# Route steps at fixed places of an attention unit: PSUM banks, product order and engine changed together

## The chip, the cores and the metric

One core of a Trainium2 chip runs the whole program. The metric is the device time of one launch in microseconds (us); lower is better. Engines are named as the profile names them: PE (TensorE, products; PEld its weight loads), DVE (VectorE), ACT (ScalarE), POOL (GpSimd), SP (SyncE, which here issues transfers). Each runs its own instructions in program order.

## What is computed

Three blocks follow each other (the reference, cut):

```python
# 1 attention: 2 batches, 8 heads, 768 positions, head size 64
keep = is_global | is_local                    # 8 global keys, 96 local ones
scores = where(keep, scale*q@k.T + bias, -1e9)
a = exp(scores - max); a = a / (sum(a) + 1e-09)
x = a @ v
# 2 a sequential route and one of 8 experts for each token
fresh_e = argmax(logits[b, s])
e = fresh_e if s == 0 or local_gate < 0.5 else prev_e
out[b, s] = softmax(logits)[e] * (relu(x @ w1[e]) @ w2[e])
# 3 real part of a 2-D FFT, norm and a two-layer MLP
```

The expert of a token can be that of the token before it, so the route of a tile of 128 positions needs the last state of the tile before.

## The kernel before

**Units.** Attention runs in `fast_attention` as 24 units, `n` = 0 to 23: six tiles `i` of 128 queries, two batches `b`, two groups `g` of four heads, `n = 4i + 2b + g`. A unit has at most 256 keys. Its work is spread over four rounds of the main loop. Round `n` issues in this order: `out(n-2, 1)` (ACT copies the second half of the turned probabilities, L165), `keep(n-3)` (DVE copies the values' sums from PSUM, L178), `scores(n)` (PE, L132), `rowmin(n)` (DVE, four L141), `upright(n-3)` (PE, L183: two products that turn the sums upright and give the gate logits), `norm(n-3)` (DVE, L195 to L201), `step` (slot 0), `transp(n-1, 0)` (PE, L159), `expo(n)` (ACT, four L150), `out(n-1, 0)`, `step` (slot 1), `transp(n-1, 1)`, `step` (slot 2), `values(n-2)` (PE, L173), `step` (slot 3). Where this text says unit `n`, the stretch from the start of `scores(n)` on PE to that of `scores(n+1)` is meant.

**Route.** After the fourth unit of a tile, `norm` adds the generator `Route.run` to the background. Each `step` advances every background generator to its next `yield`, so the number of `yield`s alone decides in which slot a route step is issued, and it does so for all but the last tile while later units run. The steps are: sum of the logits (`lg`, L465), maximum and index (L490, L493), gate masks `gn` and `gf` (L491, L497), two products that turn them into rows (L501, L502, into `rp`), ACT copy of the rows (L508), exponentials and their sum (L503, L505), a scan along the tokens (`ex`, L512), the one-hot `oh` (L517), a counting scan (`cu`, L521), products for the counts of other tiles (`other`, L531, L532), the rank `rk` (L539), two products for the places (`pp`, L544, L545), their cast (`pos`, L549), a store of the rows to memory on SP (L552) and on POOL two indirect scatters of the token list (L553). Tile 3 goes on: SP reads the first 128 list entries (L564), POOL gathers their rows with an indirect DMA (`x0`, L567).

**PSUM.** `values` writes columns 256 to 511 of the bank `sm` (`turned`); `rp` is in columns 0 to 255 of that bank. `upright` writes columns 0 to 295 of the bank `mi` (`back`); `other` and `pp` are in columns 304 to 310 of `mi`. The recording layer orders accesses of one bank's tile.

**Splits.** Four generators `Ring.take` (table `TAKES`) split expert weights into two parts while units 12 to 24 run: for each 128x512 piece ACT casts it (L991) and POOL subtracts (L993, `eng=lambda: G`). There are 16 pieces.

**Afterwards.** `early` runs an MLP for the 128 gathered tokens on PE (L825, L839 to L855) while the last tile's route ends; then lists are read and the experts start (L1088).

Of the kernel before, what the change touches and what calls it, by code (L numbers as in the profile page):

```python
# [11 lines left out]
F32 = mybir.dt.float32  # L12
# [5 lines left out]
AF = mybir.ActivationFunctionType  # L18
ALU = mybir.AluOpType
# [4 lines left out]
P = 128  # L24
B, H, S, D = 2, 8, 768, 64
E, F = 8, 1024
DM = H * D
NT = S // P
# [12 lines left out]
GATE = -1.5 * 2.0 ** -23  # L41
# [19 lines left out]
def fast_attention(tc, st, io, route):  # L61
    nc = tc.nc
    V, A, G, T = nc.vector, nc.scalar, nc.gpsimd, nc.tensor
    KS = 3
    HP = B * H // 2
    with ExitStack() as ctx:
# [79 lines left out]
        def expo(n):  # L146
            u = live[n]
            u.den = wk.tile([P, 4], F32, name="den", bufs=4)
            for x in range(4):
                A.activation(u.t[:, x, :u.W], u.t[:, x, :u.W], AF.Exp, bias=u.nm[:, x:x + 1], scale=-1.0, accum_out=u.den[:, x:x + 1])  # L150

# [35 lines left out]
        def norm(n):  # L187
# [69 lines left out]
        def step(k):  # L257

            for at, g, lo, hi in TAKES:
                if k == at:  # L260
                    bg.add(st.ring.take("e", g, cols=512, follow=False, part=(lo / 4, hi / 4), eng=lambda: G))
            bg.step()
            for _ in range(AHEAD.get(k, 0)):
                next(ahead, None)

        for n in range(N + 3):
# [35 lines left out]
            if ok(n - 1):  # L302
                transp(n - 1, 1)
            step(k + 2)
            if ok(n - 2):
# [8 lines left out]
        for k in range(4 * 3, max(AHEAD) + 1):  # L314
            step(k)
            if k == LOAD:
                st.ring.load(PIECES)
        bg.drain()
        for _ in ahead:
# [104 lines left out]
class Route:  # L424
    def __init__(self, tc, st, io):
        self.tc, self.st, self.io = tc, st, io

    def pools(self, ctx, turn=True):
# [19 lines left out]
    def run(self, i, xs, parts=None):  # L448
# [10 lines left out]
        rp = sm[:16, :256]  # L459
        pp = mi[:, 304:304 + B]  # L460
        other = mi[:16, 308:309]
        from2, from1 = st.pairs[:16, 0:16], st.pairs[:16, 16:32]
# [3 lines left out]
        else:  # L466
# [8 lines left out]
            A.copy(lg, lp)  # L475
        yield
        l8 = lg[:, :, :E]
# [18 lines left out]
        V.tensor_tensor(pe, l8, m8[:, :, :1].to_broadcast([P, B, E]), op=ALU.subtract)  # L496
# [5 lines left out]
        T.matmul(rp[:, P:2 * P], gf.rearrange("p b e -> p (b e)"), self.identb, start=True, stop=True)  # L502
        A.activation(pe, pe, AF.Exp)  # L503
        yield
        V.tensor_reduce(out=su, in_=pe, op=ALU.add, axis=AX.X)  # L505
        yield
        rows = sb.tile([16, P], F32, name="rows")
        A.copy(rows, rp[:, :P])  # L508
        V.tensor_scalar(su, su, 1e-9, None, op0=ALU.add)
        yield  # L510
        ex = sb.tile([16, P], F32, name="ex")
        V.tensor_tensor_scan(ex, rows, rp[:, P:], 0.0 if i == 0 else st.pe[:, P - 1:],  # L512
                             op0=ALU.mult, op1=ALU.add)
        V.reciprocal(su, su)
        yield
        oh = sb.tile([16, P], F16, name="oh")
        V.tensor_scalar(oh, ex, st.eid, None, op0=ALU.is_equal)  # L517
        yield
        cu = sb.tile([16, P], F32, name="cu")
# [3 lines left out]
        st.pe, st.pc = ex, cu  # L523
        yield
        if i < NT - 1:

            yield
            yield

        if i > 0:  # L530
            T.matmul(other, from2, before[:, P - 1:], start=True, stop=False)  # L531
        T.matmul(other, from1, cu[:, P - 1:], start=i == 0, stop=True)  # L532
        if i == NT - 3:
            less = mi[:1, 310:311]
# [3 lines left out]
        yield  # L538
        V.scalar_tensor_tensor(rk, cu, other, oh, op0=ALU.add, op1=ALU.mult)  # L539
        for b in range(B):  # L540
            V.tensor_scalar(xs[b][:, DM:DM + E], pe[:, b], su[:, b], None, op0=ALU.mult)
        yield
        yield
        T.matmul(pp, rk, st.sel, start=True, stop=False)  # L544
        T.matmul(pp, oh, st.base, start=False, stop=True)  # L545
        yield
        yield
        pos = sb.tile([P, B], I32, name="pos")
# [1260 lines left out]
```

## Time and profile before

| | |
|---|---|
| median of 3 runs | 680.07 us (678.15 to 684.28) |
| the profiled execution: its own time | 676.13 us |
| its span, first to last instruction | 674.2 us |
| PE / DVE / ACT / POOL busy | 627.2 / 400.3 / 279.4 / 88.4 us |
| TensorE clock granted, mean | 0.981 |

A line of the page's groups names source line, engine, operation, output and input, sizes and count, then busy time, mean of one, and the idle time in front with what ended it. A timeline row has the start from the span's beginning, the duration, the engine, line, operation and in brackets the idle time in front of it and its releaser. Instructions of one engine overlap at their ends, so the step from start to start is what one costs.

### The profile page before, as it was taken

How to read it: one execution, taken by the hardware profiler on the slowest of the kernel's cores; microseconds unless marked ns; L12 is line 12 of the kernel's file. 1: busy time of each engine (PE TensorE's matmuls, PEld its weight loads, DVE VectorE, ACT ScalarE, POOL GpSimd, SP SyncE). 2: the span in 40 equal slices, each digit the busy share in tenths (PEclk: the TensorE clock that was granted, in tenths of full speed). 3: DMA queues.
4: the chain of work that ended last, by engine and by line, in shares of the span. 5: the costliest groups of instructions: out<-in, count | busy, mean ns of one | idle time of the engine just before them, and what ended most of it. 6: DMA issues, size and time to landing. Idle time of an engine off the chain costs nothing.

```text
span 674.2 us, 9953 instructions
## 1 busy us (share of the span) xinstructions
PE 627.2 (93%) x3621; PEld 511.7 (76%) x3622; DVE 400.3 (59%) x939; ACT 279.4 (41%) x562; POOL 88.4 (13%) x100
## 2 busy tenths in 40 slices
PE   8987877687999999999999899999999999999997
PEld 3665665457899889888777688777778888888886
DVE  3767777732986598866158986989641141244112
ACT  6766668212655566655343453442211131131110
POOL 0003334423043213231010000000000000000000
PEclk8999999896999999999999999999999999999999
DMA  8332344316888887896144134245010010100001
GB/s 305 130 113 79 129 135 90 113 39 250 290 290 333 321 273 258 339 367 214 64 175 173 35 113 165 92 163 181 1 64 0 1 63 1 63 0 1 0 1 62
DMA packets 25217, 92.47 MB, mean 137 GB/s; under 512 B 7660, under 2 KB 8812, under 8 KB 17216
## 3 DMA queue, kind: packets, MB, share of 16 engines
q1 hardware_dynamic: 19408, 77.44, 33.3%
q0 software_dynamic: 4736, 10.56, 4.2%
q10 hardware_dynamic: 1008, 3.65, 1.5%
q8 instruction: 35, 0.57, 0.4%
q14 instruction: 30, 0.25, 0.1%
HBM read 81.03 MB, written 14.84 MB: 142 GB/s over the span
## 4 chain that ended last, share of the span: by engine, by line
PE 38%; DVE 11%; ACT 2%; issue 1%; DMA 1%; DVEq 0%; ACTq 0%
PE h L1621 16%; PE acc L1637 5%; PE acc L1635 5%; PE acc L1636 5%; DVE dec L1017 1%; DVE dec L1019 1%; PE y L1126 1%; PE more L1176 1%; PE more L1126 1%; PE h L1176 1%; DVE dec L1015 1%; DVE dec L1013 1%; DMA u<-x 1%; PE f L1587 1%; DVE wide L971 1%
## 5 line engine op out<-in xcount | busy, mean ns | idle before, releaser
L1626 DVE SCALAR_TENSOR_TENSOR hl<-h,hh 128x512 fp32r<-128x512 f32 x48 | 33.1, 689 | 118.5 <-ACT hh L1625 118.5
L1625 ACT ACTIVATE hh<-h 128x512 fp32r<-128x512 f32 x48 | 28.7, 597 | 153.8 <-PE h L1621 153.7
L993 DVE TENSOR_TENSOR wide<-raws,wide 128x1024 fp32r<-128x1024 f32 (+1 forms) x38 | 45.0, 1200 | 24.2 <-ACT wide L991 23.9
L150 ACT ACTIVATE t<-t,nm 128x256 f32<-128x256 f32 (+1 forms) x96 | 45.9, 480 | 21.9 <-DVE nm L141 21.8
L991 ACT CAST wide<-raws 128x1024 fp32r<-128x1024 f32 (+2 forms) x46 | 43.3, 957 | 6.1 <-PE acc L1637 3.4
L1621 PE MATMUL h<-un0h,wide 128*128 128x512 f32 (+1 forms) x136 | 42.4, 378 | 0.1
L141 DVE CUSTOM_DVE_ANT_0 t<-sp,bias 128x256 f32<-128x256 f32 (+1 forms) x96 | 32.8, 398 | 9.9 <-PE sp L132 7.9
L1636 PE MATMUL acc<-wide,hh 128*128 128x512 f32 x96 | 37.7, 393 | 0.0
L1635 PE MATMUL acc<-wide,hh 128*128 128x512 f32 x96 | 37.7, 393 | 0.0
L1637 PE MATMUL acc<-wide,hl 128*128 128x512 f32 x96 | 37.5, 391 | 0.0
L173 PE MATMUL sm<-p,vs 128*64 128x128 f32 x352 | 25.7, 288 | 5.3 <-ACT rows L508 5.3
L1149 ACT ACTIVATE hh<-h 128x512 fp32r<-128x512 f32 x28 | 16.7, 597 | 31.1 <-PE h L1146 23.2
L1621 PEld LDWEIGHTS h<-un0h,wide 128*128 128x128 f32 x136 | 25.0, 188 | 5.0 <-ACT un0h L1397 0.3
L1146 PE MATMUL h<-xh,wide 128*128 128x256 f32 x192 | 28.4, 284 | 0.4 <-DVE hl L1150 0.3
L165 ACT COPY p<-tp 128x512 f32<-128x512 f32 (+1 forms) x48 | 24.8, 538 | 8.5 <-PE tp L159 8.5
L1056 POOL DMA_INDIRECT xg<-xs,ent x23 | 25.8, 1120 | 15.9 <-issue 6.1
L173 PEld LDWEIGHTS sm<-p,vs 128*64 128x64 f32 x352 | 19.7, 142 | 9.9 <-ACT rows L508 6.5
L1146 PEld LDWEIGHTS h<-xh,wide 128*128 128x128 f32 x192 | 25.5, 192 | 1.2 <-ACT sl5h L991 0.5
L1150 DVE SCALAR_TENSOR_TENSOR hl<-h,hh 128x512 fp32r<-128x512 f32 x28 | 19.2, 686 | 11.9 <-ACT hh L1149 9.7
L159 PE MATMUL tp<-consts,t 128*128 128x128 f32 x176 | 25.7, 287 | 0.2
L1621 PE MATMUL h<-un0l,wide 128*128 128x512 f32 (+1 forms) x68 | 25.6, 377 | 0.0
L183 PE MATMUL mi<-iw,o 128*128 128x148 f32 x96 | 18.8, 320 | 5.9 <-DVE o L178 5.0
(447 smaller groups left out, 1665.7 us busy)
## 6 DMA issues: line engine op xcount, KB each, us to landing
raws<-we SPq DMA_DIRECT2D x30, 1024.0 KB
raws<-wm SPq DMA_DIRECT2D x17, 1024.0 KB
raws<-wmf SPq DMA_DIRECT2D x7, 1024.0 KB
wmf<-dec POOLq DMA_DIRECT2D x8, 512.0 KB
xs<-xrow SPq DMA_DIRECT2D x12, 260.0 KB
vs<-v SPq DMA_DIRECT2D x6, 512.0 KB
raws<-kq SPq DMA_DIRECT2D x3, 1024.0 KB
u<-x SPq DMA_DIRECT2D x6, 512.0 KB
```

The costliest lines, as they stand in the source:

```text
L141: V.tensor_tensor_reduce(out=u.t[:, x, :u.W], in0=u.sp[:, j, k, :u.W], in1=bias[:, 4 * u.g + x, u.b0:u.b0 + u.W], scale=-0.125, scalar=3.0 ...
L150: A.activation(u.t[:, x, :u.W], u.t[:, x, :u.W], AF.Exp, bias=u.nm[:, x:x + 1], scale=-1.0, accum_out=u.den[:, x:x + 1])
L173: T.matmul(turned[j * D:j * D + D, k], vs[:, ti % KS, u.h + 2 * k + j], u.p[:, 2 * k + j, c], start=c == 0, stop=c == len(tiles) - 1)
L991: (first or nc.scalar.copy)(hi[:, cs], raw[:, cs])
L993: (eng() if callable(eng) else eng or nc.vector).tensor_tensor(lo[:, cs], raw[:, cs], hi[:, cs].bitcast(F32), op=ALU.subtract)
L1146: T.matmul(ps[:, u], w[:, f], x[:, k], start=n == 0, stop=n == 11)
L1621: nc.tensor.matmul(ps[:, c], a[:, k], x[:, k, c], start=n == 0, stop=n == 11)
L1625: nc.scalar.activation(hh, ps, AF.Relu)
L1626: nc.vector.scalar_tensor_tensor(hl, ps, 0.0, hh.bitcast(F32), op0=ALU.max, op1=ALU.subtract)
L1635: T.matmul(acc[c], hh[:, cs], h2, start=first, stop=False)
L1636: T.matmul(acc[c], hh[:, cs], l2, start=False, stop=False)
L1637: T.matmul(acc[c], hl[:, cs], h2, start=False, stop=last)
```

## The change

It does five things. `upright(n-3)` and `norm(n-3)` are issued behind `transp(n-1, 1)` instead of behind `scores(n)` (except in the last two rounds). `pp`, `other` and `less` lie in the bank `sm` (columns 0 to 6) instead of `mi`. Route steps name a slot to be issued in (`at`, `to`), except those of the last tile; both row products' results are copied by one ACT copy right behind the products. Six small steps go from DVE to POOL: the `+ 1e-9` of the attention's denominators (once a unit), and for all tiles but the last `gn`, the subtraction for `pe`, the `+ 1e-9` of `su` and the two scalings of `xs`. The 16 subtractions of the splits go from POOL to DVE.

```diff
         def expo(n):
...
+            G.tensor_scalar(u.den, u.den, 1e-9, None, op0=ALU.add)
...
-            V.tensor_scalar(rs, u.den.unsqueeze(2), 1e-9, None, op0=ALU.add)
-            V.reciprocal(rs, rs)
+            V.reciprocal(rs, u.den)
...
-                    bg.add(st.ring.take("e", g, cols=512, follow=False, part=(lo / 4, hi / 4), eng=lambda: G))
+                    bg.add(st.ring.take("e", g, cols=512, follow=False, part=(lo / 4, hi / 4)))
+            route.slot = k % 4
...
-            if ok(n - 3):
+            if ok(n - 3) and not ok(n - 1):
                 upright(n - 3)
                 norm(n - 3)
...
                 transp(n - 1, 1)
+                if ok(n - 3):
+                    upright(n - 3)
+                    norm(n - 3)
...
+    def at(self, s, n=1):
+
+        for _ in range(1 if s is not None else n):
+            yield
+        while s is not None and self.slot not in (None, s):
+            yield
...
-        pp = mi[:, 304:304 + B]
-        other = mi[:16, 308:309]
+        pp = sm[:, 0:B]
+        other = sm[:16, 4:5]
+        last, soon = i == NT - 1, i in (NT - 3, NT - 2)
+        X = V if last else G
+        to = lambda s, n=1: self.at(None if last else s, n)
...
-        V.tensor_scalar(gn, z.to_broadcast([P, B, E]), GATE, None, op0=ALU.is_ge)
+        X.tensor_scalar(gn, z.to_broadcast([P, B, E]), GATE, None, op0=ALU.is_ge)
...
-        yield
-        yield
+        yield from to(0, 2)
         T.matmul(rp[:, 0:P], gn.rearrange("p b e -> p (b e)"), self.identb, start=True, stop=True)
...
+        if not last:
+            A.copy(rows, rp)
...
+        X.tensor_scalar(su, su, 1e-9, None, op0=ALU.add)
...
-        yield
-        if i < NT - 1:
-
-            yield
-            yield
-
+        yield from to(3)
         if i > 0:
             T.matmul(other, from2, before[:, P - 1:], start=True, stop=False)
...
-        yield
-        yield
+        yield from to(3, 2)
         T.matmul(pp, rk, st.sel, start=True, stop=False)
```

Three places in the program, as the order of instructions has them. First PE in unit 13, before: `scores`, the two `upright` products (L183), the route's `other` (L531, L532), the transposes, the values.

```order
L132 MATMUL sp<-raws 128x256 x4
L183 MATMUL mi<-iw,o 128x148 [waits DVE_49]
L183 MATMUL mi<-iw,o 128x148
L531 MATMUL mi<-cu,consts 16x1 [waits DVE_49]
L532 MATMUL mi<-cu,consts 16x1
L159 MATMUL tp<-consts,t 128x128 [waits Activation_49]
```

The same unit on PE after (L184 is `upright`, L174 the values, L546 and L547 are `other`):

```order
L132 MATMUL sp<-raws 128x256 x4
L160 MATMUL tp<-consts,t 128x128 [waits Activation_49]
L160 MATMUL tp<-consts,t 128x128 x3
L160 MATMUL tp<-consts,t 128x128 [waits Activation_49]
L160 MATMUL tp<-consts,t 128x128 x3
L184 MATMUL mi<-iw,o 128x148 [waits DVE_49]
L184 MATMUL mi<-iw,o 128x148
L174 MATMUL sm<-p,vs 64x128 x8
L546 MATMUL sm<-cu,consts 16x1
L547 MATMUL sm<-cu,consts 16x1 [waits DVE_49]
```

`other` moved from the second place of the unit to its end and out of the bank that `upright` writes; `upright` moved behind the transposes.

Second DVE in unit 13, behind the four L141, before (L539 is `rk`, L541 the scaling of `xs`, L178 the next `keep`):

```order
L195 TENSOR_SCALAR rs<-den 128x4
L196 RECIPROCAL rs<-rs 128x4 [waits DVE_49]
L199 TENSOR_TENSOR lgp<-mi,rs 128x40 [waits DVE_49,PE_49]
L201 TENSOR_TENSOR xrow<-mi,rs 128x256
L539 SCALAR_TENSOR_TENSOR rk<-cu,mi,oh 16x128 [waits PE_49]
L541 TENSOR_SCALAR xrow<-pe,su 128x8 x2
L178 COPY o<-sm 128x256 [waits PE_49]
```

And after (L541 is now `cu`, L1009 a split, L555 `rk`, L179 `keep`):

```order
L541 SCALAR_TENSOR_TENSOR cu<-consts,cu,oh 16x128 [waits DVE_49]
L1009 TENSOR_TENSOR sl0l<-raws,sl0h 128x512 [waits DMAHW6_49,Activation_49]
L196 RECIPROCAL rs<-den 128x4
L199 TENSOR_TENSOR lgp<-mi,rs 128x40 [waits DVE_49,PE_49]
L201 TENSOR_TENSOR xrow<-mi,rs 128x256
L555 SCALAR_TENSOR_TENSOR rk<-cu,sm,oh 16x128 [waits PE_49]
L1009 TENSOR_TENSOR sl0l<-raws,sl0h 128x512 [waits Activation_49]
L179 COPY o<-sm 128x256
```

Two splits and the counting scan joined the unit; the small addition and the two scalings left it.

Third POOL around unit 22, before (L553 are tile 3's scatters, L567 the gather of `x0`, L993 splits, L104 a patch of keys):

```order
L553 DMA list<-dest,pos 12416x2 [waits DVE_49]
L553 DMA list<-dest,pos 12416x2
L993 TENSOR_TENSOR wide<-raws,wide 128x512 [waits Activation_49]
L993 TENSOR_TENSOR wide<-raws,wide 128x512 [waits DMAHW4_49,Activation_49]
L104 COPY kq<-gk 128x4x8 [waits PE_49]
L567 DMA vs<-xs,ent_89 128x520 [waits DMAHW3_49,DMAHW5_49,DMAHW2_49,DMAHW6_49,DMAHW1_49,DMAHW7_49,DMAHW0_49,DMASW0_49]
L993 TENSOR_TENSOR wide<-raws,wide 128x512 [waits Activation_49] x3
```

And after (L569 the scatters, L151 the denominators' addition of units 22 and 23, L583 the gather, L508 `gn`, L513 `pe` and L528 `su` of tile 4):

```order
L569 DMA list<-dest,pos 12416x2 [waits DVE_49]
L569 DMA list<-dest,pos 12416x2
L151 TENSOR_SCALAR den<-den 128x4 [waits Activation_49,Pool_49]
L583 DMA vs<-xs,ent_89 128x520 [waits DMAHW4_49,DMAHW3_49,DMAHW5_49,DMAHW2_49,DMAHW6_49,DMAHW1_49,DMAHW7_49,DMAHW0_49,DMASW0_49]
L508 TENSOR_SCALAR gn<-lg 128x16 [waits DVE_49]
L513 TENSOR_TENSOR pe<-lg,m_1489 128x16 [waits DVE_49]
L104 COPY kq<-gk 128x4x8 [waits PE_49]
L151 TENSOR_SCALAR den<-den 128x4 [waits Activation_49,Pool_49]
L528 TENSOR_SCALAR su<-su 128x2 [waits DVE_49]
```

Behind the gather stood splits; now tile 4's `gn`, `pe` and `su` stand there.

## Rows read from the trace of the kernel before

**Rows 1.** The page, busy time of the engines over the span:

```profile
PE 627.2 (93%) x3621; PEld 511.7 (76%) x3622; DVE 400.3 (59%) x939; ACT 279.4 (41%) x562; POOL 88.4 (13%) x100
```

**Rows 2.** Windows: length, then busy by engine, clock, DMA share, GB/s:

```profile
core 0: us, PE busy (x) PEld busy (x) DVE busy (x) ACT busy (x) POOL busy (x), PEclk, DMA share, GB/s
27.31:30.98 3.67, 3.67 (x39) 2.95 (x37) 2.67 (x15) 3.01 (x11) 0.00 (x0) 1.00 0.04 3
27.31:88.76 61.45, 48.61 (x472) 38.38 (x470) 44.37 (x221) 42.16 (x137) 12.95 (x17) 0.97 0.28 89
88.76:129.95 41.19, 29.48 (x306) 23.51 (x305) 32.27 (x135) 24.71 (x76) 17.71 (x18) 0.99 0.42 103
...
130.00:136.00 6.00, 5.14 (x16) 3.75 (x16) 4.03 (x22) 1.05 (x3) 2.00 (x2) 0.50 0.75 240
```

**Rows 3.** Waits: engine and tile, releaser, us in total, times, longest:

```profile
PE mi L531 <- DVE xrow L201: 9.2, 4, 2.8
...
PE sm L173 <- ACT rows L508: 5.3, 5, 1.1
```

**Rows 4.** Timeline of unit 6, a unit with no route step on PE:

```profile
27.31 1.13 PE L132 MATMUL sp<-raws 64*128 64x256 f32 x8
...
28.38 0.77 PE L183 MATMUL mi<-iw,o 128*128 128x148 f32 x4
28.63 0.43 DVE L141 CUSTOM_DVE_ANT_0 t<-sp,bias 128x256 f32<-128x256 f32 x1 [0.78 <-PE sp L132]
...
28.98 1.04 PE L159 MATMUL tp<-consts,t 128*128 128x128 f32 x8
29.10 0.51 ACT L150 ACTIVATE t<-t,nm 128x256 f32<-128x256 f32 x1 [0.66 <-DVE nm L141]
...
29.95 0.85 PEld L173 LDWEIGHTS sm<-p,vs 128*64 128x64 f32 x16 [0.17 <-issue]
...
31.08 0.56 ACT L165 COPY p<-tp 128x512 f32<-128x512 f32 x1
```

**Rows 5.** Timeline of unit 17, POOL, DVE and PE:

```profile
84.22 1.26 POOL L993 TENSOR_TENSOR sl1l<-raws,sl1h 128x512 fp32r<-128x512 f32 x1
...
84.32 1.19 DVE L195 TENSOR_SCALAR rs<-den 128x4 f32<-128x4 f32 x1
...
86.41 0.20 PE L531 MATMUL mi<-cu,consts 16*16 16x1 f32 x2 [2.85 <-DVE xrow L201]
```

**Rows 6.** Timeline from tile 3's places to the early MLP:

```profile
113.23 0.15 DVE L549 CAST pos<-mi 128x2 int32<-128x2 f32 x1
...
113.67 1.00 POOL L553 DMA_INDIRECT list<-dest,pos  x1 [3.34 <-DVE cu L561]
...
114.97 0.97 POOL L553 DMA_INDIRECT list<-dest,pos  x1 [0.30 <-issue]
...
115.64 0.22 PE L501 MATMUL sm<-identb,gn 128*16 128x128 bf16 x1
...
119.73 0.33 SPq L564 DMA_DIRECT2D ent<-list  x1
...
123.64 1.07 POOL L567 DMA_INDIRECT vs<-xs,ent  x1 [5.03 <-issue]
...
124.73 3.71 POOL L993 TENSOR_TENSOR wide<-raws,wide 128x512 fp32r<-128x512 f32 x3
...
125.31 3.28 DVE L539 SCALAR_TENSOR_TENSOR rk<-cu,mi,oh 16x128 f16<-16x128 f32 x1 [0.34 <-PE mi L532]
...
129.95 0.90 PEld L825 LDWEIGHTS tp<-consts,vs 128*128 128x128 f32 x4
```

**Rows 7.** Groups by line and form: DVE's scans and large splits, POOL's small copies:

```profile
L521 DVE TENSOR_TENSOR_SCAN cu<-consts,cu,oh 16x128 f32<-16x128 f32 x4 | 1.9, 472 | 0.1
...
L993 DVE TENSOR_TENSOR wide<-raws,wide 128x1024 fp32r<-128x1024 f32 (+1 forms) x38 | 45.0, 1200 | 24.2 <-ACT wide L991 23.9
...
L104 POOL COPY raws<-gk 128x32 f32<-128x32 f32 x6 | 1.3, 210 | 32.0 <-PE sp L132 32.0
```

More of the change, by code (lines that the diff above doesn't have):

```diff
@@ L147, in expo @@
             u = live[n]
[L148 removed]
+            u.den = wk.tile([P, 4, 1], F32, name="den", bufs=4)
             for x in range(4):
[L150 removed]
+                A.activation(u.t[:, x, :u.W], u.t[:, x, :u.W], AF.Exp, bias=u.nm[:, x:x + 1], scale=-1.0, accum_out=u.den[:, x])
+            G.tensor_scalar(u.den, u.den, 1e-9, None, op0=ALU.add)
         def transp(n, k):
@@ L317, in fast_attention @@
                 st.ring.load(PIECES)
+        route.slot = None
         bg.drain()
@@ L426, in __init__ @@
         self.tc, self.st, self.io = tc, st, io
+        self.slot = None
+    def at(self, s, n=1):
[3 more added lines that the diff above has]
+            yield
     def pools(self, ctx, turn=True):
@@ L475, in run @@
             A.copy(lg, lp)
-        yield
+        if not soon:
+            yield from to(3)
         l8 = lg[:, :, :E]
@@ L490, in run @@
             V.max(m8[:, b], l8[:, b])
-        V.tensor_scalar(gn, z.to_broadcast([P, B, E]), GATE, None, op0=ALU.is_ge)
+        X.tensor_scalar(gn, z.to_broadcast([P, B, E]), GATE, None, op0=ALU.is_ge)
         for b in range(B):
             V.max_index(ix[:, b], m8[:, b], l8[:, b])
-        yield
+        yield from to(3 if soon else 1)
         V.tensor_copy(fr, ix[:, :, :1])
-        V.tensor_tensor(pe, l8, m8[:, :, :1].to_broadcast([P, B, E]), op=ALU.subtract)
+        X.tensor_tensor(pe, l8, m8[:, :, :1].to_broadcast([P, B, E]), op=ALU.subtract)
         V.scalar_tensor_tensor(gf, z.to_broadcast([P, B, E]), GATE, fr.to_broadcast([P, B, E]),
                                op0=ALU.is_lt, op1=ALU.mult)
-        yield
-        yield
+        yield from to(0, 2)
         T.matmul(rp[:, 0:P], gn.rearrange("p b e -> p (b e)"), self.identb, start=True, stop=True)
         T.matmul(rp[:, P:2 * P], gf.rearrange("p b e -> p (b e)"), self.identb, start=True, stop=True)
+        rows = sb.tile([16, 2 * P], F32, name="rows")
+        if not last:
+            A.copy(rows, rp)
         A.activation(pe, pe, AF.Exp)
-        yield
+        yield from to(1)
         V.tensor_reduce(out=su, in_=pe, op=ALU.add, axis=AX.X)
-        yield
-        rows = sb.tile([16, P], F32, name="rows")
-        A.copy(rows, rp[:, :P])
-        V.tensor_scalar(su, su, 1e-9, None, op0=ALU.add)
-        yield
+        if last:
+            yield
+            A.copy(rows[:, :P], rp[:, :P])
+        X.tensor_scalar(su, su, 1e-9, None, op0=ALU.add)
+        if last:
+            yield
         ex = sb.tile([16, P], F32, name="ex")
-        V.tensor_tensor_scan(ex, rows, rp[:, P:], 0.0 if i == 0 else st.pe[:, P - 1:],
+        V.tensor_tensor_scan(ex, rows[:, :P], (rp if last else rows)[:, P:], 0.0 if i == 0 else st.pe[:, P - 1:],
                              op0=ALU.mult, op1=ALU.add)
+        yield from to(2)
         V.reciprocal(su, su)
-        yield
         oh = sb.tile([16, P], F16, name="oh")
         V.tensor_scalar(oh, ex, st.eid, None, op0=ALU.is_equal)
-        yield
+        yield from to(1)
         cu = sb.tile([16, P], F32, name="cu")
@@ L523, in run @@
         st.pe, st.pc = ex, cu
-        yield
-        if i < NT - 1:
-            yield
-            yield
+        yield from to(3)
         if i > 0:
@@ L533, in run @@
         if i == NT - 3:
-            less = mi[:1, 310:311]
+            less = sm[:1, 6:7]
             T.matmul(less, st.pairs[:, 48:49], st.pairs[:, 49:50], start=True, stop=False)
```

12 lines of the change are left out of this document (6 added, 6 removed).

## The prediction

> **What bounds the kernel now.** I read the page first: PE is busy 93% of the span [rows 1], so a change pays where PE waits. The windows come next. Unit 6 (27.31 to 30.98) is PE without a hole: 3.67 us long, 3.67 busy, while DVE needs 2.67 and ACT 3.01 [rows 2]. So 3.67 us is the floor of a unit. But the twelve units 6 to 17 (27.31 to 88.76) take 61.45 us instead of 12 x 3.67 = 44.0, and from unit 18 to the early MLP (88.76 to 129.95) 29.48 us of PE fill only 41.19 [rows 2]. The waits say what sits in these holes: `other` (L531) waited 9.2 us in 4 times for `norm`'s last reader of its bank, the values (L173) 5.3 us in 5 times for ACT's copy of the route's rows [rows 3]. The timeline shows a second layer: in unit 17 DVE's tiny L195 begins at 84.32 and lasts until POOL's split, begun at 84.22, ends at 85.48; `norm` is late by that, and `other` after 2.85 us of waiting starts at 86.41 [rows 5].
>
> **First term, units 6 to 17.** The change takes all three causes away. `other` and `pp` leave `norm`'s bank and stand at the unit's end; the rows are copied right behind their products, ahead of ACT's exponentials, a unit's length before the values can be held by them; no 1.27 us subtraction is left on POOL. What PE keeps is 12 x 3.67 = 44.0 plus the route's own products. The first of two row products takes 0.22 and `other` 0.20 [rows 5, 6]; with `pp` estimated at no more than that, about 0.5 a tile, 1.4 for the parts of three tiles here.
>
> What is late next is DVE. From unit 12 on it gets 16 splits at 0.6 (half of 1.20 for twice the columns [rows 7]; the row itself bounds one at 0.6 to 1.2). Unit 13 holds two splits, `cu` at 0.47 [rows 7] and `rk`, estimated the same: about 2.5 of plain unit work (2.67 less the small addition) + 1.2 + 0.95 = 4.65, a microsecond over PE's 3.67. Unit 12 overruns too: there DVE's reciprocal of `su` waits for POOL's addition, queued behind the denominators' step, which waits for the unit's last exponential. In unit 6 the exponentials begin 1.79 us in and make way for the copy at 3.77 [rows 4], so that addition is done at about 4.2 and delays the next unit's first DVE work by 0.7. Cover: in unit 6 the values start 2.64 us in [rows 4]; with `upright` moved, the transposes stand 0.77 us earlier, so what ACT's copies and exponentials have in hand shrinks by that, to about 0.6. Walking units 12 to 15 through in order (late by 0.7, 1.1, 1.0, caught up in unit 15, which has no split), PE waits about 1.2 us in them and 0.6 in 16 and 17. Sum: 44.0 + 1.4 + 1.8 = 47.2, a gain of 14.3. Bounds: 16.1 without a late DVE; if DVE set the pace in all of units 12 to 17, at some 4.65, the gain falls to 10.2.
>
> **Second term, unit 18 to the early MLP.** Here I expect no gain. Two POOL orders hurt. Tile 3's `pe` (now POOL) stands behind tile 2's two scatters, which take 1.00 + 0.30 + 0.97 [rows 6]; ACT's exponential of `pe` waits for it and unit 19's four exponentials stand behind that on ACT. With `gf` one slot later than the row products want it, I count about 1.1 + 1.2 us of PE waiting in units 19 and 20.
>
> The larger one: tile 4's `gn` and `pe` stand on POOL behind the gather of `x0`. Before, that gather started at 123.64, 10.4 us after tile 3's places (113.23): scatters until 115.94, list read at 119.73, gather 3.91 later. POOL did nothing meanwhile, idle 5.03 us with splits ready, which ran only at 124.73 [rows 6]. So its wait holds POOL's queue. After, `gn` comes some 11.7 us behind tile 3's places (10.4 + 1.07 + 0.2, the last the small copy's 0.21 [rows 7]). On PE the row products that need `gn` come in unit 23 right behind its scores: from the places, late in unit 21, that is the rest of that unit, all of unit 22 and 1.1 of scores, about 4.1. PE stands still for 11.7 - 4.1 = 7.6 us. Behind it the exponentials of unit 23 wait for ACT's `pe`, and DVE's `su`, `ex`, reciprocal and two splits for those, so `upright(21)` waits once more, about 1.3. Counted from unit 18's start: units 18 to 20 with waits 14.8, 21 and 22 with 0.9 over 8.1, scores and standstill to 31.6, then rest of unit 23, unit 24's products, two more uprights and the values behind DVE's copies 11.6: 43.2, against 41.19 [rows 2]. Against that stand the stalls that vanish here: 3.28 us of DVE's `rk` behind POOL's last three splits [rows 6] and others like it; they are why the loss is 2.0 and no more. Bounds: with no standstill 43.2 - 7.6 = 35.6 (a gain of 5.6); with the gather as slow again behind other traffic, a few us more.
>
> **Third term, after 129.95.** From 130 to 136 PE runs at a granted clock of 0.50, 1.2 GHz, busy 5.14 of 6.00 [rows 2], after a stretch in which it mostly waited for that `rk`. The last tile's route passes through these products. At full clock half of 5.14, 2.6, would be saved at most; nothing if the wait in unit 23 brings the dip here again. I take 0.8, since the route beside it has its own DVE steps. Nothing later changes; it all moves forward.
>
> **Sum.** 14.3 - 2.0 + 0.8 = 13.1 us off. From the profiled execution's own 676.13 (span 674.2 and 1.9 around it) that is 663. The median of the runs shown is 680.07, 3.9 above that execution; a difference carries over better than a level, so I forecast 667.
>
> A rule that speaks against the change is in the Trainium skill, SBUF — State Buffer, section Who interferes with whom: a VectorE instruction with two SBUF inputs and a GpSimd instruction that reads SBUF hold each other out, whichever starts first. By it the splits, now on DVE, hold POOL's small steps up to 0.6 each; where DVE or PE then waits for such a step (three tiles), that would add 1.8, and the result 669. The trace of before shows only the reverse, DVE behind POOL [rows 5, 6].
>
> **Rivals.** (a) The gather does not hold the small steps, because its wait ends sooner once scatters start earlier or transfers are idle. For it: most of the 10.4 us is landing time of transfers, which can vary. Against: the idle 5.03 us [rows 6]. Gain 13.1 + 7.6 = 20.7: 659. (b) DVE sets the pace in all units with splits, 12 to 23, not only in the worst. For it: 44.37 us of DVE in the twelve units [rows 2] before it gets the splits. Against: the small steps leave it, and much of that sum is time held by POOL. Six units lose 4.1 us more by the bound above and six others perhaps 2: 667 + 6 = 673. (c) Slower: POOL's 49 small steps (24 denominators, 25 of the route) each hold a DVE instruction for their whole length, as one split held L195 [rows 5]. At the small copy's 0.21 that is 10.3 us at most, if none hides; it decides from 13.1 / 49 = 0.27 a step on. At 0.5, 24.5 us are lost against 13.1 gained: 680.07 + 11.4 = 691. For it: no small arithmetic of POOL stands in the trace; against: copies of 32 columns at 0.21 [rows 7], and DVE has over a microsecond free in units without splits. (d) Gains and standstill cancel, because the standstill also drops the clock for the early MLP: the 2.6 us of the third term are lost and not gained and the rest of rival (b) joins: 676.
>
> **Chances.** Forecast 0.50, (a) 0.18, (b) 0.18, (c) 0.06, (d) 0.08. A measurement of this kernel tells about 1%, 6.8 us, from no change; the line for faster is 673.3. The forecast, (a) and half of (b) and some lie below it: 0.80. The other half of (b) less a little and (d) lie within: 0.13; slower 0.07. The range reaches to (a) below, 658, and past (b) above, 675; (c) and most of (d) are left out.
>
> **What would show it.** Right: between units 6 and 17 unit pitches of 3.7 to 4.3 with no PE wait over 0.5 for `norm` or rows; in unit 23 a PE wait of 6 to 9 us in front of the row products, released by POOL; POOL's gather in front of it after several idle us; no DVE instruction of 128x4 longer than 0.4. Wrong: no such PE wait (rival a); DVE without idle time from unit 12 to 23 (rival b); small POOL steps over 0.3 us with DVE rows stretched to their ends (rival c). If the stretch to unit 18 is not shorter by 10 us or more, the first term is wrong.

## The result, and the profile after

The changed kernel takes 658.62 us, median of 4 runs (657.13 to 660.04), against 679.11 (676.48 to 684.28) of the kernel before beside it: ratio 0.9689, 95% interval 0.9624 to 0.9754. The profiled execution took 660.04 with a span of 658.3, mean granted clock 0.983. The forecast was 667 with a range down to 658: faster as said, but by 20.5 between the medians where 13.1 had been worked out.

The page's busy line, to be held against [rows 1]:

```profile
PE 622.8 (95%) x3621; PEld 509.3 (77%) x3622; DVE 392.3 (60%) x906; ACT 279.3 (42%) x562; POOL 83.0 (13%) x133
```

The same products are there (x3621); 15.9 us of span are gone and PE's busy time fell by only 4.4, so it is mostly waiting that went. The windows [rows 2], here unit 6, units 6 to 17, unit 18 to the early MLP (now L841), and the first 6 us of that MLP, in the same columns:

```profile
26.19:29.81 3.62, 3.62 (x39) 2.92 (x38) 2.67 (x14) 3.05 (x11) 0.22 (x1) 1.00 0.00 0
26.19:72.51 46.32, 45.92 (x471) 36.65 (x469) 39.53 (x195) 40.34 (x133) 12.64 (x38) 1.00 0.39 120
72.51:115.49 42.98, 31.54 (x309) 24.66 (x307) 30.04 (x132) 26.57 (x80) 11.64 (x28) 0.92 0.43 96
115.30:121.30 6.00, 4.51 (x18) 3.35 (x18) 4.16 (x21) 1.06 (x3) 1.57 (x2) 0.72 0.99 180
```

The twelve units went from 61.45 to 46.32, and PE is busy for all but 0.4 of it, at a granted clock of 1.00. The next stretch ends here with the first product of the early MLP on PE (115.49). [rows 2] ended with its first weight load (129.95); up to the first product, at 130.19, the kernel before took

```profile
88.76:130.19 41.43, 29.72 (x306) 23.73 (x305) 32.27 (x135) 24.71 (x76) 17.71 (x18) 0.99 0.42 104
```

so it grew from 41.43 to 42.98, and 11.4 us of holes are left in it. All windows below end at that product. The waits of PE, longest first, against [rows 3]:

```profile
PE sm L517 <- POOL gn L508: 6.9, 1, 6.9
PE xtp L1104 <- issue: 3.1, 1, 3.1
PE f L1603 <- issue: 2.2, 1, 2.2
PE more L50 <- issue: 2.0, 1, 2.0
PE tp L160 <- ACT p L166: 1.9, 4, 1.0
```

Both entries of [rows 3] are gone, and one new one of 6.9 leads. Unit 13 on PE, which holds the two splits, against unit 17 of [rows 5]:

```profile
52.18 1.13 PE L132 MATMUL sp<-raws 64*128 64x256 f32 x8
53.25 1.12 PE L160 MATMUL tp<-consts,t 128*128 128x128 f32 x8
54.29 0.77 PE L184 MATMUL mi<-iw,o 128*128 128x148 f32 x4
54.99 1.09 PE L174 MATMUL sm<-p,vs 128*64 128x128 f32 x16
56.02 0.20 PE L546 MATMUL sm<-cu,consts 16*16 16x1 f32 x2
```

No row has a bracket: `other` (L546) follows the values without a wait. The new wait lies in unit 23; POOL from tile 3's scatters on, against [rows 6], and PE's row:

```profile
93.14 1.05 POOL L569 DMA_INDIRECT list<-dest,pos  x1 [0.51 <-DVE cu L577]
94.49 0.97 POOL L569 DMA_INDIRECT list<-dest,pos  x1 [0.30 <-issue]
96.91 0.22 POOL L151 TENSOR_SCALAR den<-den 128x4 f32<-128x4 f32 x1 [1.44 <-ACT t L150]
102.67 1.11 POOL L583 DMA_INDIRECT vs<-xs,ent  x1 [5.54 <-DMA ent<-list]
103.81 0.28 POOL L508 TENSOR_SCALAR gn<-lg 128x16 bf16<-128x16 f32 x1
104.04 0.23 POOL L513 TENSOR_TENSOR pe<-lg,m 128x16 f32<-128x16 f32 x1
```

```profile
104.14 0.28 PE L517 MATMUL sm<-identb,gn 128*16 128x128 bf16 x1 [6.94 <-POOL gn L508]
```

POOL stands idle 5.54 us in front of the gather, whose list is still being read, and `gn`, a step of 0.28, comes behind it. From the first scatter to `gn` it is 10.67. PE waits 6.94, and the clock falls in that wait: half clock is granted from 100.25 to 107.08, so that the transposes behind it take 1.97 us, where unit 13 has 1.12.

Last, POOL's small additions and DVE's first split, against [rows 7]. The first row is a group (24 of them, mean 224 ns); the others are a moment of unit 13:

```profile
L151 POOL TENSOR_SCALAR den<-den 128x4 f32<-128x4 f32 x24 | 5.4, 224 | 64.3 <-ACT t L150 64.2
```

```profile
53.21 0.69 DVE L1009 TENSOR_TENSOR sl0l<-raws,sl0h 128x512 fp32r<-128x512 f32 x1
...
53.39 0.58 POOL L104 COPY raws<-gk 128x32 f32<-128x32 f32 x1 [0.52 <-PE sp L132]
```

The additions cost 0.22 each. By the same groups `gn`, `pe` and `su` cost 0.28, 0.22 and 0.23, a scaling 0.36. The copy, 0.21 in [rows 7], began under a split of DVE and lasted until that ended: the hold between the two engines exists in this direction too, but no PE row behind it shows a wait.

### The profile page after: what moved, and what is told of

Read it like the earlier page. It is cut to its first block, busy times and chain, and to the rows that moved or that the text cites. A ratio compares the mean times of both kernels' runs of the same rounds, so it can differ in the third digit from the quotient of the medians.

```text
span 658.3 us, 9969 instructions
## 1 busy us (share of the span) xinstructions
PE 622.8 (95%) x3621; PEld 509.3 (77%) x3622; DVE 392.3 (60%) x906; ACT 279.3 (42%) x562; POOL 83.0 (13%) x133
## 4 chain that ended last, share of the span: by engine, by line
PE 39%; DVE 11%; ACT 2%; issue 1%; DMA 1%; DVEq 0%; ACTq 0%
PE h L1637 17%; PE acc L1653 5%; PE acc L1652 5%; PE acc L1651 5%; DVE dec L1033 1%; DVE dec L1035 1%; PE y L1142 1%; PE more L1192 1%; PE more L1142 1%; PE h L1192 1%; DVE dec L1031 1%; DVE dec L1029 1%; DMA u<-x 1%; PE f L1603 1%; DVE wide L987 1%
## 5 line engine op out<-in xcount | busy, mean ns | idle before, releaser
L1009 DVE TENSOR_TENSOR wide<-raws,wide 128x1024 fp32r<-128x1024 f32 (+2 forms) x46 | 50.5, 1111 | 25.8 <-ACT wide L1007 25.7
L141 DVE CUSTOM_DVE_ANT_0 t<-sp,bias 128x256 f32<-128x256 f32 (+1 forms) x96 | 32.7, 395 | 6.7 <-ACT p L166 2.9
L1072 POOL DMA_INDIRECT xg<-xs,ent x23 | 27.5, 1196 | 15.7 <-issue 6.1
L160 PE MATMUL tp<-consts,t 128*128 128x128 f32 x176 | 27.2, 290 | 2.4 <-ACT p L166 1.9
L160 PEld LDWEIGHTS tp<-consts,t 128*128 128x128 f32 x176 | 19.6, 144 | 11.0 <-ACT p L166 6.6
L174 PE MATMUL sm<-p,vs 128*64 128x128 f32 x352 | 24.5, 279 | 0.0
L1035 DVE SCALAR_TENSOR_TENSOR dec<-raws,dec 128x1024 int32<-128x1024 int32 x18 | 22.0, 1225 | 0.6
```

The lines of the kernel that those rows point to most:

```text
L141: V.tensor_tensor_reduce(out=u.t[:, x, :u.W], in0=u.sp[:, j, k, :u.W], in1=bias[:, 4 * u.g + x, u.b0:u.b0 + u.W], scale=-0.125, scalar=3.0 ...
L160: T.transpose(u.tp[k][:, j, c], u.t[:, 2 * k + j, c * P:(c + 1) * P], st.ident)
L1009: (eng() if callable(eng) else eng or nc.vector).tensor_tensor(lo[:, cs], raw[:, cs], hi[:, cs].bitcast(F32), op=ALU.subtract)
```

## The experiments

Fifteen runs were made: eleven edited kernels, the changed kernel once more, and the kernel before three times. Runs 1 to 4 were taken on one chip, 5 to 8, 9 to 12 and 13 to 15 each on another. The median of the kernel before differs between these sessions (679 to 682 in most, 675.64 beside the last of the edited kernels), so windows of the traces are compared first and ratios only with the session in mind. "Early MLP" is its first transpose in each kernel.

**1 and 2. The standstill.** The changed kernel, with tile 4's small steps on DVE:

```diff
-        X = V if last else G
+        X = V if i >= NT - 2 else G
```

> The changed kernel with tile 4's small route steps (gn, pe, su, the two scalings) back on DVE; nothing else. Theory (the gather holds POOL's queue, PE stands still 6.9 us in unit 23 and the whole program is late by that): the wait in front of unit 23's row products falls under 1.5 us, the early MLP starts 5 to 7 us earlier counted from unit 18, and the time falls by 5 to 7 us against the changed kernel, to about 652. Rival (the last tile's chain or the gathered rows set the end anyway): the wait goes, but the experts' start counted from unit 18 and the time move by less than 1.5 us.

and with those of tiles 3 and 4:

```diff
-        X = V if last else G
+        X = V if last or soon else G
```

> As e1, for tile 3 too. Theory (tile 3's pe stands behind tile 2's two scatters on POOL and holds ACT): of the 2.4 us of PE waits in units 19 and 20 the part before unit 20's transposes (0.98) goes, that before unit 19's row products (1.38, for DVE) stays, so 0.5 to 1.5 us less than e1. Rival (DVE is full there and the five steps put back, 0.17 each, cost as much): the same as e1 within 0.5 us or slower.

Measured: 653.95 (653.32 to 655.56) and 653.57 (652.76 to 655.18), ratios 0.965 [0.9587, 0.9713] and 0.9638 [0.9574, 0.9702]. Unit 18 to the early MLP, first in 1 and then in 2:

```profile
72.25:110.53 38.28, 31.49 (x309) 24.77 (x307) 30.33 (x137) 26.57 (x80) 10.83 (x23) 0.96 0.47 108
```

```profile
72.13:108.92 36.79, 31.03 (x309) 24.76 (x307) 30.75 (x142) 26.48 (x80) 8.87 (x18) 0.95 0.52 112
```

PE's row product in experiment 1, and the gather, which has not moved:

```profile
99.04 0.22 PE L517 MATMUL sm<-identb,gn 128*16 128x128 bf16 x1 [2.14 <-DVE o L179]
```

```profile
102.11 1.11 POOL L583 DMA_INDIRECT vs<-xs,ent  x1 [5.29 <-DMA ent<-list]
```

The queue behind the gather is the cause: off it, the wait falls from 6.94 to 2.14 and the stretch from 42.98 to 38.28. It does not vanish, because DVE's own steps are late next: the wait stays over the 1.5 that was expected. So the standstill was worth 4.7, not its whole length. Tile 3's steps give 1.5 more to the early MLP, of which 0.4 is left in the medians, which is within the noise. As expected, the wait in unit 20 goes and that in unit 19 stays. In the trace of 2 half clock is granted behind the start of the early MLP (110.9 to 114.3); that this takes the rest is not shown.

**3 and 4. What each engine move is worth.** The changed kernel with the splits back on POOL (3):

```diff
-                    bg.add(st.ring.take("e", g, cols=512, follow=False, part=(lo / 4, hi / 4)))
+                    bg.add(st.ring.take("e", g, cols=512, follow=False, part=(lo / 4, hi / 4), eng=lambda: G))
```

and with all six small steps back on DVE (4):

```diff
-            G.tensor_scalar(u.den, u.den, 1e-9, None, op0=ALU.add)
...
-            V.reciprocal(rs, u.den)
+            V.tensor_scalar(rs, u.den, 1e-9, None, op0=ALU.add)
+            V.reciprocal(rs, rs)
...
-        X = V if last else G
+        X = V
```

> The changed kernel with the 16 subtractions of the splits back on POOL. Theory (a POOL subtraction of 1.27 us holds DVE's small instructions and POOL's own small steps queue behind it): DVE's L196 or L537 again has rows over 1 us, PE waits in units 12 to 17 grow by 3 to 6 us, time 4 to 8 us over the changed kernel. Rival (DVE's load in units with splits is what costs, POOL has room): DVE's work per unit falls by 0.6 to 1.2, unit pitches in 12 to 17 return to 3.7 to 3.9, and the time falls by 1.5 to 3 us.

> The changed kernel with all six kinds of small steps back on DVE (denominators' addition in norm, gn, pe, su, scalings); places, bank and splits stay. Theory (the small steps on POOL buy DVE about 0.2 us a unit and 0.85 a tile, but their queue costs the standstill): no wait of unit 23 for POOL, 5 to 7 us gained there; units 12 to 17 longer by 0.5 to 2 us through the fuller DVE; together 3 to 6 us under the changed kernel, slower than e2 by 0.5 to 2.5. Rival (units 6 to 17 became fast because DVE was relieved): these units lose 4 us or more, and the time is that of the changed kernel or above.

Measured: 3 is 660.81 (660.06 to 662.63), 0.975 [0.9685, 0.9814]; 4 is 657.42 (656.09 to 658.13), 0.9687 [0.9624, 0.975]. In 3 DVE is still held by POOL's splits, as in this row pair of unit 19, but only in a few places (between unit 6 and the early MLP four small rows of DVE last over a microsecond):

```profile
77.28 1.27 POOL L1009 TENSOR_TENSOR sl1l<-raws,sl1h 128x512 fp32r<-128x512 f32 x1
...
77.51 1.06 DVE L512 CAST fr<-ix 128x2 f32<-128x2 uint32 x1
```

Neither expectation of 3 met. Its median is 1.2 to 2.2 us over the changed kernel's two medians (658.62, and 659.57 in experiment 9), too little to be sure of across sessions, and its windows do not bear it out. Units 6 to 17 and the rest to the early MLP:

```profile
26.87:72.70 45.83, 45.10 (x470) 36.54 (x468) 36.86 (x192) 40.45 (x134) 18.30 (x43) 1.00 0.39 121
72.70:116.13 43.43, 31.18 (x310) 25.01 (x307) 27.16 (x119) 26.05 (x80) 25.46 (x39) 0.88 0.45 95
```

With the splits on POOL the twelve units are 0.5 us shorter than in the changed kernel, and the stretch behind lies between the 42.98 of that kernel and the 44.72 of its other execution (9). So no gain of the splits' move shows in these windows: it costs a little in units 6 to 17, once the order and the bank are changed. In 4, the same two windows:

```profile
26.18:73.14 46.96, 46.09 (x471) 36.63 (x469) 42.19 (x219) 40.34 (x133) 6.01 (x10) 1.00 0.38 116
73.14:112.58 39.44, 31.34 (x310) 24.84 (x308) 32.64 (x154) 26.48 (x80) 6.43 (x9) 0.96 0.46 104
```

The small steps on POOL gain 0.6 in units 6 to 17 (46.96 against 46.32) and cost 3.5 in the stretch behind (39.44 against 42.98). They are a good move in the first and a bad one in the second. The expectation of 4 had the direction of both right, but of 3 to 6 us under the changed kernel only 1.2 came.

**5 and 6. One part alone, on the kernel before.** The bank of `pp`, `other` and `less` (5); the splits on DVE (6, the edit of 3 the other way round):

```diff
-        pp = mi[:, 304:304 + B]
-        other = mi[:16, 308:309]
+        pp = sm[:, 0:B]
+        other = sm[:16, 4:5]
...
-            less = mi[:1, 310:311]
+            less = sm[:1, 6:7]
```

> The kernel before with pp, other and less in the bank sm; nothing else. Theory (other waits for norm because it shares norm's bank): the four waits of other for L201, 9.2 us together, go, the values' waits for ACT's rows (5.3 us) stay; what is late next costs 1 to 3 us of it: 6 to 9 us under the kernel before. Rival (the wait moves: DVE is as late, and pp or the values wait for the rank or for norm in its place): under 3 us gained.

> The kernel before with the 16 subtractions on DVE. Theory (POOL's subtractions hold small DVE instructions, and other and the last rank product wait for those): L195 rows over 0.5 us and the 3.28 us of the rank vanish, units 13, 17 and 21 lose 0.8 to 1.2 us each, the last units 2 to 4: 3 to 7 us under the kernel before. Rival (DVE gets 16 x 0.6 us more, which delays norm as much): within 2 us of the kernel before. The run with splits back on POOL in the changed kernel (2 us slower, no long rows on the path) speaks for the rival only where steps have fixed places.

Measured: 675.75 (674.57 to 677.66), ratio 0.9932 [0.9901, 0.9964], and 674.3 (672.68 to 675.74), ratio 0.9895 [0.9838, 0.9952], the kernel before at 681.75. The waits of 5, on PE:

```profile
PE sm L173 <- ACT rows L508: 6.9, 5, 1.5
PE sm L173 <- DVE rk L539: 4.7, 3, 1.9
PE sm L173 <- DVE pos L549: 4.3, 3, 1.4
```

and of 6:

```profile
PE mi L183 <- DVE o L178: 10.5, 10, 2.1
PE mi L531 <- DVE xrow L201: 5.6, 4, 1.9
```

Each part alone turns one wait into another. In 5 the values now share a bank with `rk` and `pos` and wait for those (9.0 us) where 9.2 for `norm` had been; units 6 to 17 shorten only from 61.45 to 59.44, and the stretch behind grows from 41.43 to 45.45. In 6 no small DVE step lasts over 0.2 longer than usual any more, `other` waits 5.6 and not 9.2, but `upright` waits for the copy of the values behind the splits; units 6 to 17 take 61.6. Going by the windows both rivals held, the wait that moves and the DVE that is as late. Both medians are 6 to 7 us under the kernel before all the same, though the profiled spans, 674.9 and 673.1, hardly differ from 674.2: that difference lies in executions without a profile (13 to 15 take this up).

**7, 8 and 12. Bank and order of products.** The changed kernel with the bank `mi` (7, the edit of 5 the other way round), with `upright` and `norm` back behind the scores (8); and the kernel before with the new bank and the new place of `upright` together, without slots and engine moves (12):

```diff
-            if ok(n - 3) and not ok(n - 1):
+            if ok(n - 3):
                 upright(n - 3)
                 norm(n - 3)
...
-                if ok(n - 3):
-                    upright(n - 3)
-                    norm(n - 3)
```

> The changed kernel with pp, other and less back in the bank mi. Theory (the bank is what counts: products behind the values now wait for norm's readers, late by DVE): PE waits 0.4 to 1.3 us in front of other and pp, nine times: 4 to 9 us over the changed kernel. Rival (the fixed places alone suffice, norm is done when slot 3 comes): within 1.5 us of it.

> The changed kernel with upright and norm back behind the scores. Theory (DVE's copy keep is late in units with splits, and the later place is its cover): units 13, 14, 15, 17, 18, 19 wait 0.5 to 1.2 us for keep: 3 to 6 us over the changed kernel. Rival (what upright loses, the transposes win, which stand 0.77 us later again and wait less for ACT): within 1.5 us.

> The kernel before with pp, other and less in the bank sm and upright and norm behind the transposes; no slots, no other engine. Theory (without fixed places the route's readers of the bank, rank, places and rows, hold the values): the waits for norm and keep go, waits of the values for L539, L549 and L508 stay, 1.4 to 1.9 us each: units 6 to 17 take 55 to 58 us, time 6 to 10 us under the kernel before. Rival (bank and order of the products are all of it, the places do nothing): units 6 to 17 take under 50 us, time within 4 us of the changed kernel.

Measured: 661.46 (660.06 to 663.25), 666.52 (665.44 to 667.1) and 663.5 (659.72 to 665.1); ratios 0.9714 [0.9658, 0.977], 0.9779 [0.9725, 0.9832] and 0.9788 [0.9722, 0.9853]. Units 6 to 17, in this order, and for 12 the stretch behind them:

```profile
26.76:75.37 48.61, 45.52 (x470) 36.59 (x468) 40.51 (x198) 41.73 (x136) 13.34 (x41) 1.00 0.37 114
```

```profile
27.43:78.25 50.82, 46.31 (x471) 36.86 (x469) 40.35 (x197) 41.15 (x136) 13.43 (x39) 1.00 0.36 109
```

```profile
25.90:75.01 49.11, 45.85 (x470) 36.70 (x469) 41.80 (x217) 40.71 (x135) 12.78 (x16) 1.00 0.35 111
75.01:117.90 42.89, 33.69 (x308) 27.30 (x306) 33.49 (x140) 26.04 (x78) 18.03 (x18) 0.84 0.42 105
```

In 7, `other` is back at waiting for L201 (2.5 us in 2 waits). In 8, PE's longest entry is:

```profile
PE mi L184 <- DVE o L179: 19.4, 14, 8.7
```

The bank is worth 2.3 in the twelve units and the place of `upright` 4.5, each on top of the rest; `upright` early waits for the copy of the sums 14 times. (By the medians, on another chip than the changed kernel's, 7 is 2.8 over it, between its two expectations, and 8 is 7.9 over it, more than either.) Together, and with nothing else of the change (12), they take 12.3 of the 15.1 us, and the median lies 3.9 from the changed kernel's beside it: the rival of 12 held, not its theory. From unit 18 on that kernel gains nothing (42.89 against 41.43), with a clock of 0.84 there. One hold stands out: in tile 4's route a cast of two columns, 0.17 in most rows of the changed kernel, lasts until POOL's two splits, with a small copy between them (99.24 to 101.87), have ended.

```profile
99.02 2.88 DVE L498 CAST fr<-ix 128x2 f32<-128x2 uint32 x1
```

**9, 10 and 11. The changed kernel again, the gather later, and two edits joined.** 9 has no edit. 10 puts two more `yield`s ahead of the gather, so that `gn` and `pe` are issued ahead of it; 11 is 2 and 3 together:

```diff
             yield
             yield
+            yield
+            yield
             G.indirect_dma_start(...)
```

> The changed kernel once more, beside the three that follow, to read them against it on one chip. Theory (the medians differ by more than the two profiled executions because the kernel before mostly runs with a lower mean clock than in its profiled execution): 657 to 661 at a mean clock of 0.982 to 0.988, the kernel before at 0.962 to 0.985 and slower where it is lower. Rival (the extra gain is chance of the first runs): the ratio comes to 0.975 to 0.98.

> The changed kernel with the gather two slots later in the program, behind tile 4's gn and pe on POOL; engines as in the changed kernel. Theory (it is the queue, not the engine of the small steps): the 6.9 us in front of unit 23's row products go; now unit 23's denominators and tile 4's su stand behind the gather, DVE's reciprocal of su waits for them and keep behind it, so part comes back as a wait of upright in unit 24: 2 to 5 us under the changed kernel, e1 stays better. Rival (a small step on POOL is slow or late in itself): the wait for gn stays over 4 us.

> e2 (small steps of tiles 3 and 4 on DVE) with the splits on POOL. Theory (with the small steps out of POOL's queue DVE's load is what makes unit 19's and 23's row products wait, 1.4 and 2.1 us): both waits fall under 1 us, time 1 to 3 us under e2, about 651.5. Rival (three splits behind the gather hold DVE for 3.7 us as in the kernel before): a row of DVE over 2 us in the last units, time as e2 or up to 3 us over it.

Measured: 659.57 (658.29 to 660.75), 656.12 (653.14 to 657.36) and 654.9 (650.47 to 659.76), the kernel before at 675.64 (673.95 to 680.13) on the chip then; ratios 0.9733 [0.9676, 0.9789], 0.9682 [0.962, 0.9743] and 0.9686 [0.9602, 0.9769]. In 9 units 6 to 17 take 46.34, as before, but the stretch behind them is longer than in the first execution:

```profile
72.15:116.87 44.72, 32.34 (x309) 25.59 (x307) 30.12 (x132) 26.69 (x80) 11.68 (x28) 0.89 0.40 92
```

The standstill is 8.00 there and not 6.94, and POOL's idle time in front of the gather 6.60 and not 5.54. The ratio lies between the first session's and the 0.975 at which the rival of 9 began. POOL in 10:

```profile
97.11 0.25 POOL L508 TENSOR_SCALAR gn<-lg 128x16 bf16<-128x16 f32 x1 [0.28 <-DVE lg L481]
...
103.82 1.13 POOL L585 DMA_INDIRECT vs<-xs,ent  x1 [6.07 <-ACT p L166]
```

`gn` runs 6.7 us earlier on the same engine, the gather starts 1.15 later, and PE's wait is again 2.14: another way to the same finding as 1, with the engine unchanged. Part comes back as a wait of `upright`, 2.41 at 106.92, as expected; the median is 3.5 us less than the changed kernel's beside it. The theory of 11 failed: PE waits 5.0 us in 3 times in front of row products, where 2 has 3.5 in 2. Its runs lie 9.3 apart, and whether it beats 2 stays open; its profiled span of 650.4 is the shortest seen.

**13 to 15. Where the kernel before loses its clock.** The kernel before, unedited, three times with a profile (the two later expectations repeat the first).

> The kernel before, unchanged, to see where its clock falls in an execution other than the one shown. Theory (the change removes the dips): where the mean clock is under 0.978, the stretches at half clock that the first profile lacks lie ahead of about 160 us, in attention, the early MLP or the list stage, where this kernel's TensorE waits and the changed one's does not; the half-clock time ahead of 160 us is then over 27 us, against 23.9 in the first profile. Rival (chance of the session): they lie behind 160 us, in the experts and the MLP, where both kernels issue the same products; ahead of 160 us the sum stays at 24 us within 3.4.

> A second look at the kernel before, with the same two expectations: theory, half-clock time ahead of 160 us over 27 us wherever the mean clock is under 0.978; rival, the added half-clock time lies behind 160 us.

> A third look at the kernel before, with the same two expectations: theory, half-clock time ahead of 160 us over 27 us wherever the mean clock is under 0.978; rival, the added half-clock time lies behind 160 us.

Measured: 679.82, 676.46 and 676.61, at mean clocks of 0.974, 0.982 and 0.981. Up to and behind 152 us, 13 first, then 14:

```profile
0.00:152.00 152.00, 120.27 (x987) 89.78 (x989) 98.00 (x474) 88.32 (x292) 37.99 (x53) 0.92 0.40 125
152.00:674.00 522.00, 508.84 (x2636) 424.86 (x2634) 301.05 (x464) 191.59 (x270) 51.15 (x47) 0.99 0.39 139
```

```profile
0.00:152.00 152.00, 120.22 (x996) 87.85 (x997) 99.79 (x476) 89.12 (x293) 38.93 (x54) 0.96 0.40 126
152.00:674.00 522.00, 507.13 (x2627) 423.55 (x2625) 300.76 (x463) 190.64 (x269) 49.24 (x46) 0.99 0.39 141
```

And 13 in two of its stretches at half clock:

```profile
82.00:90.00 8.00, 6.69 (x51) 5.88 (x52) 2.57 (x11) 2.74 (x8) 1.66 (x2) 0.57 0.16 31
106.00:113.00 7.00, 5.66 (x40) 4.73 (x42) 2.20 (x12) 3.55 (x10) 1.64 (x2) 0.52 0.19 78
```

Ahead of 152 us the clock is 0.92 against 0.96: 23.9 us at 1.2 GHz against 13.7. Behind it both show 0.99. The expectation had set 160 us and over 27, and by that it was missed: ahead of 160 it is 26.4 against 20.3 in the first profile, within what the rival allowed. (The 23.9 given there for the first profile is its sum up to 164.) The line at 160 cuts through a stretch at half clock that every profile of this kernel has (153.4 to 163.6 in the first, 157.5 to 167.7 in 13). At 152, ahead of that stretch, the theory's direction shows, but this line was chosen after the result.

The stretch at 82 begins in unit 17; in the 10 us before it PE was busy 6.99. There PE waits 2.85 for `norm`, as in the first profile, but then works on at half clock, and the unit takes 8.85 us, not 7.06. Where the time goes by stage shows in the start of unit 6 and the lengths of three stretches, from PE's rows, all in us:

| profile | unit 6 starts | units 6 to 17 | 18 to early MLP | from there to the end | its own time |
|---|---|---|---|---|---|
| before, first | 27.31 | 61.45 | 41.43 | 543.98 | 676.13 |
| before, 13 | 25.76 | 61.69 | 47.80 | 542.58 | 679.82 |
| before, 14 | 27.55 | 61.37 | 41.91 | 543.67 | 676.46 |
| before, 15 | 25.80 | 59.91 | 45.26 | 543.68 | 676.61 |
| changed, first | 26.19 | 46.32 | 42.98 | 542.79 | 660.04 |
| changed, 9 | 25.81 | 46.34 | 44.72 | 542.11 | 660.75 |

The stretch from unit 18 to the early MLP is what varies most. In 13 it is 6.4 longer than in the first profile:

```profile
87.45:135.25 47.80, 34.63 (x307) 28.05 (x306) 31.64 (x135) 24.23 (x74) 16.77 (x17) 0.86 0.37 89
```

The same products (x307, against x306 in the line of the first profile) keep PE busy for 34.63 us and not 29.72, at a clock of 0.86 and not 0.99; only 1.5 is added waiting. In 15 it is a wait: PE stands 5.41 us for `norm` in unit 21, where 2.85 was the first profile's. So one execution with a low mean clock shows what half clock costs there. Those at 0.962 to 0.972, which some timed runs had, were not profiled.

## Why the steps of the prediction held and its sum failed

*The first term held, its parts less well.* 47.2 forecast, 46.3 measured, with unit pitches of 3.61 to 4.45 and no wait over 0.3. A unit without route work now takes 3.62, not 3.67: over twelve units that is 0.6 of the 0.9 missed. Of the 1.8 of waiting for a late DVE hardly 0.4 came, and PE's work beyond twelve such units is 2.5, not 1.4; these two misses nearly cancel. Of the gain of 15.1, 1.5 is half clock in the first profile (64.65 to 68.06, in unit 13, which takes 8.58 there and 7.04 in 13). Against the four profiles of the kernel before the gain is 13.6 to 15.4, around the 14.3 forecast. Of the three causes that the term removes, POOL's splits under DVE cost nothing by themselves any more once the other two are gone (experiment 3).

*The second term held in its mechanism.* 43.2 forecast, 42.98 measured; a standstill of 7.6 forecast, 6.94 measured, on the engine, at the instruction and for the reason given. Experiments 1 and 10 show the reason. That the length fits to 0.2 is partly luck: the standstill was 0.7 shorter than forecast, the five units ahead of it 0.7 longer, and the changed kernel's other execution has 8.00 and 44.72. The 4.1 us that PE was to have in hand is mis-summed: unit 22 at 3.67 and the scores at 1.1 are 4.8 without any rest of unit 21. The trace has 4.8, from tile 3's places (92.41, in unit 22) to the end of the scores (97.20), and 11.7 - 4.8 is the 6.9 measured. Wrong was the bound beside it, "with no standstill 43.2 - 7.6 = 35.6": DVE was late next, and 38.28 came out. Of the two small waits, 1.38 and 0.98 are in units 19 and 20, against 1.1 and 1.2; the first was for DVE's copy of the sums.

*Rivals.* (a) fell: the gather held the queue. Its 659 is the time that came out all the same, but not by its way. (b) fell: DVE did not set the pace in units 12 to 17, where PE waits 0.3 in all. (c) fell: a step costs 0.22 to 0.36, and it needed 0.27 for each of 49, none hidden; but PE waited for none in units 6 to 17, and the one small DVE row that lasted longer there (a cast at 63.99, 0.45) ended with a scatter of POOL's, not with a small step. (d) fell: the early MLP has a clock of 0.72 in its first 6 us against 0.50. In the standstill the clock did drop, to half until 107.08, which falls on unit 23's products; the early MLP has a shorter stretch of it (117.3 to 120.7). By the Trainium skill, SBUF — State Buffer, section Who interferes with whom, POOL's small steps would be held by DVE's splits: the trace agrees for single copies (0.58 and not 0.21), but no PE wait of units 6 to 17 goes back to one, and the 1.8 that I gave for it did not appear.

*The step that failed is the last one*: "a difference carries over better than a level". The two profiled executions differ by 16.1: 15.1 in units 6 to 17, 1.1 ahead of them (not counted), less 1.55 behind them (2.0 forecast), 1.2 from the early MLP to the end (0.8 forecast as the third term), and 0.2 outside the span. That is 3.0 more than the 13.1. The largest part of it, the 1.1 ahead of unit 6, is no effect of the change: two profiles of the kernel before start unit 6 at 25.76 and 25.80, earlier than the changed kernel, and the first has half clock from 13.45 to 16.86. The medians differ by 20.5, so 4.4 more went in the carrying: 3.0 because the profiled execution of the kernel before (676.13 at a clock of 0.981) is that much under its median, and 1.4 because that of the changed kernel is its slowest of four. The level that was worked out for the profiled execution, 663, lies closer to the 660.04 that it took and to the median of 658.62 than the 667 that was forecast.

In the one low execution that was profiled, what the carried difference left out lies in the second stretch. That was priced from 41.19, and over four profiles of the kernel before that stretch takes 41.4 to 47.8. Experiment 13, whose 679.82 is close to the median, is 19.8 over the changed kernel's profiled execution: 15.4 of it in units 6 to 17 and 4.8 from unit 18 to the early MLP, where the forecast had a loss of 2.0. Its added length there is mostly half clock. So the clock was a term of attention too, beside the waits that the change removes, and I had priced it only for the early MLP. The timed runs point the same way: those of the kernel before beside experiment 5 went from 676.24 at 0.979 to 684.33 at 0.962, while the changed kernel kept to 0.981 to 0.987 in eight runs. That half clock is the cause is shown by one execution only, on another chip. How much of the 4.4 us it is in the first session stays open; in the session of experiment 9, where the kernel before ran at 0.975 to 0.984, the medians differ by 16.1.

*Which part did it.* Bank and order of the products together give 12.3 of 15.1 us in units 6 to 17; the bank alone, on the kernel before, gives 2.0 there (experiment 5). The order alone was not run on it: in the changed kernel without the bank (7) 12.8 of the 15.1 are left, so the order may be the larger part. The slots and engine moves give the remaining 2.8; as the small steps give 0.6 of it and the splits cost 0.5, the slots should be most of it, though no run has them alone. The small steps of tiles 3 and 4 on POOL lose about 5 us again behind unit 18. The lowest median measured is the changed kernel with those steps on DVE: 653.57, not to be told from the 653.95 with tile 4's alone.

## What to carry to other kernels

When several waits share one resource, a trial of one part alone can show the wait moving and look like a failure, as the bank alone did here; join the parts before judging. A small step given to an idle engine costs its place in that engine's queue, not its length: look for what waits there with nothing done, and go by the wait that is next when you price its removal. If the granted clock dips beside the waits that a change removes, take several profiles before carrying a difference from one of them to a median: here one stretch of an unchanged kernel took 41.4 to 47.8 us.

## What the runs showed that was not expected

The kernel before, unchanged, took between 673.95 and 684.33 us over the sessions, and the order of these times is nearly that of its mean clock (0.984 and 0.962 at the ends). All of the added half clock of execution 13 lay ahead of 152 us; behind it, with TensorE 97% busy, the mean was 0.99 in both.

A two-column cast of DVE lasted 2.88 us beside POOL's splits, where 0.17 is its length without them. And POOL, with 13% of the span busy, was the engine behind the longest wait of the changed kernel.
